# Decode attention on one core: scores by VectorE word transposes of K, a ring for all large loads, q computed first, output rows in PSUM

## The chip, the cores and the metric

The kernel runs on one core of a Trainium2 chip. The metric is the device time of one execution in microseconds (us), the median of several. The profile is one execution; its span runs from the first to the last instruction and is about 2 us shorter than the device time. A program on one core has no second die to compare with, so states were judged against the fastest run of the same kernel.

Engines are PE (matrix multiply; PEld is its weight load), DVE (VectorE), ACT (ScalarE), POOL (GpSimd) and SP, which issues nearly all loads. All loads share 16 DMA engines.

## The reference

Two branches work on `x` of shape 2 x 1 x 1024, and a gate mixes them. Nearly all bytes are in the K and V caches: 2 batches x 32 heads x 16384 keys x 128 numbers in bf16. That is 64 (batch, head) pairs, each with 4 MB of K and 4 MB of V.

```python
q = (x @ wq).reshape(B, 1, 32, 128).transpose(0, 2, 1, 3)
scores = einsum("bhqd,bhkd->bhqk", q, k_cache) * 128 ** -0.5
o = einsum("bhqk,bhkd->bhqd", softmax(scores), v_cache)
a = o.transpose(0, 2, 1, 3).reshape(B, 1, 4096) @ wo
# second branch b: layernorm, w1, gelu, token shift, w2, residual, layernorm, w3, gelu, w4, residual
g = sigmoid((x * gate_w).sum(-1, keepdims=True))
return g * a + (1 - g) * b
```

With one query per pair every byte is used once, so the time cannot fall below that of the loads.

## The kernel before

K, V and weight chunks have a pool each, K and V with two buffers. A pair's 128 score columns are split: 80 by multiplying K with a broadcast q on GpSimd (eight chunks of ten) or VectorE and reducing on VectorE, 48 by fp32 transposes on PE, copies on ACT and matmuls.

```python
kpool = ctx.enter_context(tc.tile_pool(name="kpool", bufs=2))
vpool = ctx.enter_context(tc.tile_pool(name="vpool", bufs=2))
# ... cut ...
def vec_qk_stage(i, c0, c1):
    for c in range(c0, c1):                       # CH = 8 columns a chunk; set-up cut
        if c % 4 == 3:
            nc.vector.tensor_tensor(out=prod[:], in0=Kn[:, j0 : j0 + CH, :], in1=in1, op=ALU.mult)
        else:
            nc.gpsimd.tensor_tensor(out=prod[:], in0=Kn[:, j0 : j0 + CH, :], in1=in1, op=ALU.mult)
        nc.vector.tensor_reduce(out=Ssb[:, j0 : j0 + CH], in_=prod[:], axis=AX.X, op=ALU.add)
# ... cut ...
# PV: 4 probability columns are the stationary operand, 512 columns of V move through
for g in range(NGV):                              # 32 times
    nc.tensor.matmul(o4[:], lhsT=Pt[:, 4 * g : 4 * g + 4],
                     rhs=Vf[:, 4 * g * Dh : (4 * g + 4) * Dh], start=(g == 0), stop=(g == NGV - 1))
```

The last three pairs use another PV: 128 matmuls, each with 128 x 128 of V as weights and one probability column. q is computed four heads at a time: every 8 pairs a chunk of `wq` is loaded and `compute_q_chunk` runs inside the pair loop. Of its matmuls, 16 have 512 columns; they make q broadcast over all partitions.

## Time and profile before

| | before |
|---|---|
| time, median | 1436.12 us (3 runs, 1434.21 to 1436.15) |
| span | 1434.6 us |
| bytes by the load queue | 572.55 MB |
| mean DMA rate over the span | 400 GB/s |
| busy: PE, VectorE, GpSimd | 72%, 78%, 81% |

The page of the kernel before: busy time (share of the span), the DMA rate in 40 equal slices, the load queue, and the chain of work that ended last.

```profile
span 1434.6 us, 21356 instructions
PE 1036.9 (72%) x8898; PEld 621.9 (43%) x8898; DVE 1124.5 (78%) x1357; ACT 289.9 (20%) x596; POOL 1167.5 (81%) x516
GB/s 380 305 430 421 416 272 436 430 427 423 421 423 422 429 418 411 377 417 428 422 345 424 423 417 423 349 412 423 432 410 359 421 422 417 414 362 418 423 429 169
q1 hardware_dynamic: 38376, 572.55, 95.0%
DVE 34%; POOL 34%; PE 18%; DMA 8%; issue 4%; ACT 2%; SPq 0%; ACTq 0%; DVEq 0%; POOLq 0%
```

Most slices stand at 410 to 436 GB/s, and from slice 17 on every fourth or fifth falls to 345 to 377. The chain is two thirds GpSimd and VectorE, and 8% DMA: compute is what loads wait for. One such dip in stretches of 5 us (start and end, length; busy us and number of instructions of PE, PEld, VectorE, ScalarE, GpSimd; granted clock, DMA share, GB/s):

```profile
185.00:190.00 5.00, 0.42 (x10) 0.38 (x10) 4.54 (x2) 0.00 (x0) 3.98 (x2) 0.50 0.99 426
190.00:195.00 5.00, 2.97 (x12) 1.47 (x11) 3.04 (x8) 0.49 (x2) 0.00 (x0) 0.50 0.28 115
195.00:200.00 5.00, 5.00 (x17) 1.66 (x16) 5.00 (x4) 0.00 (x0) 4.14 (x2) 0.66 0.00 0
200.00:205.00 5.00, 4.92 (x42) 2.81 (x41) 4.27 (x5) 1.09 (x3) 5.00 (x3) 1.00 0.38 105
```

For some 10 us nearly nothing is loaded, because no buffer is free. The queue's waits name whom SP waited for before it could issue (us in total, times, longest):

```profile
SPq L142 <- DVE prod L429: 664.4, 52, 29.7
SPq L142 <- POOL prod L431: 99.3, 56, 3.1
```

L142 is the K load. It waits for the last reader of the K buffer. A wait of SP costs nothing while earlier loads still fill the DMA engines; the dips show where it did cost. The groups that the costing uses (busy us, mean ns of one):

```profile
L431 POOL TENSOR_TENSOR prod<-Kn,qbc 128x1024 f32<-128x1024 bf16 x501 | 1163.0, 2356 | 216.9 <-DVE Ssb L432 155.9
L432 DVE TENSOR_REDUCE Ssb<-prod 128x8 f32<-128x1024 f32 x625 | 728.8, 1208 | 84.8 <-POOL prod L431 72.0
L429 DVE TENSOR_TENSOR prod<-Kn,qbc 128x1024 f32<-128x1024 bf16 x124 | 262.6, 2118 | 0.0
```

One PV in the old form (ns of one matmul: least, median, greatest; start of the first and the last), and a one-column PV of the last pairs (start, us, engine):

```profile
L504 PE MATMUL o_475<-Vn,Pt x32: 379/379/634, 39.8 to 49.0; 128*4 128x512 bf16 x32
1425.61 3.56 PE L535 MATMUL ocol_tail<-Pt,Vn 128*128 128x1 bf16 x128 [0.31 <-DVE OT L542]
```

### The profile page before, as it was taken

How to read it: one execution, taken by the hardware profiler on the slowest of the kernel's cores; microseconds unless marked ns; L12 is line 12 of the kernel's file. 1: busy time of each engine (PE TensorE's matmuls, PEld its weight loads, DVE VectorE, ACT ScalarE, POOL GpSimd, SP SyncE). 2: the span in 40 equal slices, each digit the busy share in tenths (PEclk: the TensorE clock that was granted, in tenths of full speed). 3: DMA queues.
4: the chain of work that ended last, by engine and by line, in shares of the span. 5: the costliest groups of instructions: out<-in, count | busy, mean ns of one | idle time of the engine just before them, and what ended most of it. 6: DMA issues, size and time to landing. Idle time of an engine off the chain costs nothing.

```text
span 1434.6 us, 21356 instructions
## 1 busy us (share of the span) xinstructions
PE 1036.9 (72%) x8898; PEld 621.9 (43%) x8898; DVE 1124.5 (78%) x1357; ACT 289.9 (20%) x596; POOL 1167.5 (81%) x516
## 2 busy tenths in 40 slices
PE   3547758867687677777588775886757867677777
PEld 2333434434343443444435443553534544354456
DVE  5688689778787875888859887788959888688863
ACT  1211212122121211211212221221212222121221
POOL 6798678888688785999959998699968999599960
PEclk7767767778777788888787887878878788777887
DMA  9799969999999999899989999899998999989994
GB/s 380 305 430 421 416 272 436 430 427 423 421 423 422 429 418 411 377 417 428 422 345 424 423 417 423 349 412 423 432 410 359 421 422 417 414 362 418 423 429 169
DMA packets 38473, 573.91 MB, mean 400 GB/s; under 512 B 3044, under 2 KB 11236, under 8 KB 21992
## 3 DMA queue, kind: packets, MB, share of 16 engines
q1 hardware_dynamic: 38376, 572.55, 95.0%
q8 instruction: 69, 1.13, 0.3%
q14 instruction: 28, 0.23, 0.0%
HBM read 572.53 MB, written 0.00 MB: 399 GB/s over the span
## 4 chain that ended last, share of the span: by engine, by line
DVE 34%; POOL 34%; PE 18%; DMA 8%; issue 4%; ACT 2%; SPq 0%; ACTq 0%; DVEq 0%; POOLq 0%
POOL prod L431 34%; DVE Ssb L432 21%; DMA Kn<-in_A_k_cache_dram 8%; DVE prod L429 7%; PE T L447 3%; DVE o4s L516 2%; PE misc L195 2%; PE misc L479 2%; PE misc L521 2%; ACT Pt L487 2%; DVE junk L482 1%; PE S L459 1%; DVE m L475 1%; PE ocol_tail L535 1%; PE o_475 L504 1%
## 5 line engine op out<-in xcount | busy, mean ns | idle before, releaser
L431 POOL TENSOR_TENSOR prod<-Kn,qbc 128x1024 f32<-128x1024 bf16 x501 | 1163.0, 2356 | 216.9 <-DVE Ssb L432 155.9
L432 DVE TENSOR_REDUCE Ssb<-prod 128x8 f32<-128x1024 f32 x625 | 728.8, 1208 | 84.8 <-POOL prod L431 72.0
L504 PEld LDWEIGHTS <-Pt 128*4 128x4 bf16 x1952 | 173.5, 91 | 321.9 <-issue 93.2
L447 PE MATMUL T<-ident_f,Kn 128*128 128x128 f32 x1596 | 311.9, 338 | 1.4 <-ACT KT L452 0.7
L452 ACT COPY KT<-T 128x512 f32<-128x512 f32 x384 | 221.9, 587 | 386.1 <-PE T L447 377.9
L429 DVE TENSOR_TENSOR prod<-Kn,qbc 128x1024 f32<-128x1024 bf16 x124 | 262.6, 2118 | 0.0
L447 PEld LDWEIGHTS T<-ident_f,Kn 128*128 128x128 f32 x1596 | 221.8, 173 | 14.8 <-issue 10.5
L459 PE MATMUL S<-qsel_122,KT 128*128 128x2 bf16 x3192 | 142.8, 166 | 48.1 <-ACT KT L452 40.1
L459 PEld LDWEIGHTS <-KT 128*128 128x128 bf16 x3192 | 130.1, 102 | 90.9 <-ACT KT L452 75.5
L477 ACT ACTIVATE Dm<-ident_f,m 128x128 f32<-128x128 f32 x64 | 25.7, 401 | 533.9 <-DVE m L475 533.9
L521 PE MATMUL misc<-ident_f,o4s 4*128 4x4 f32 x244 | 30.3, 226 | 142.7 <-DVE o4s L516 142.7
L521 PEld LDWEIGHTS misc<-ident_f,o4s 4*128 4x128 f32 x244 | 25.6, 177 | 160.8 <-DVE o4s L516 116.9
L514 DVE RECIPROCAL rinv<-misc 4x1 f32<-4x1 f32 x61 | 9.4, 154 | 86.9 <-PE misc L512 86.9
L479 PE MATMUL misc<-Dm,ones_f 128*128 128x128 f32 x128 | 42.7, 430 | 27.1 <-ACT Dm L477 27.1
L487 ACT ACTIVATE Pt<-Ssb,nb 128x128 bf16<-128x128 f32 x64 | 25.7, 401 | 154.4 <-DVE junk L482 154.4
L195 PE MATMUL misc<-wqc,x_rep 128*128 128x512 bf16 x128 | 44.1, 522 | 0.0
L179 PE MATMUL misc<-qT,sel 128*128 128x8 bf16 x16 | 1.6, 168 | 52.5 <-DVE qT L176 52.5
L479 PEld LDWEIGHTS misc<-Dm,ones_f 128*128 128x128 f32 x128 | 27.0, 262 | 28.1 <-ACT Dm L477 27.6
L482 DVE TENSOR_SCALAR_CACHE_REDUCE junk<-misc 128x128 f32<-128x128 f32 x64 | 18.6, 290 | 25.2 <-PE misc L479 25.2
L524 DVE TENSOR_REDUCE OT<-misc 128x1 bf16<-128x4 f32 x61 | 10.0, 164 | 36.0 <-PE misc L521 36.0
L512 PE MATMUL misc<-rs,ones_f 128*4 128x1 f32 x122 | 11.7, 165 | 33.2 <-ACT Pt L487 33.2
L316 PEld LDWEIGHTS <-wc 128*128 128x128 bf16 x576 | 17.8, 98 | 36.1 <-issue 35.5
(212 smaller groups left out, 771.2 us busy)
## 6 DMA issues: line engine op xcount, KB each, us to landing
Kn<-in_A_k_cache_dram SPq DMA_DIRECT2D x64, 4096.0 KB, 15.3
Vn<-in_A_v_cache_dram SPq DMA_DIRECT2D x64, 4096.0 KB, 22.5
wc<-in_B_w_dram SPq DMA_DIRECT2D x11, 1024.0 KB, 18.3
wqc<-in_A_wq_dram SPq DMA_DIRECT2D x8, 1024.0 KB, 25.9
woh<-in_A_wo_dram SPq DMA_DIRECT2D x32, 256.0 KB, 23.1
wc<-in_B_w_dram SPq DMA_DIRECT2D x8, 896.0 KB, 15.4
xr<-in_A_x_dram SPq DMA_DIRECT2D x1, 4.0 KB, 1.5
x_row<-in_A_x_dram SPq DMA_DIRECT2D x1, 4.0 KB
```

The costliest lines, as they stand in the source:

```text
L195: nc.tensor.matmul(qbps[:], lhsT=x_rep[:, b, kc, :], rhs=wqc[:, kc, :], start=(kc == 0), stop=(kc == KC - 1),)
L429: nc.vector.tensor_tensor(out=prod[:], in0=Kn[:, j0 : j0 + CH, :], in1=in1, op=ALU.mult)
L431: nc.gpsimd.tensor_tensor(out=prod[:], in0=Kn[:, j0 : j0 + CH, :], in1=in1, op=ALU.mult)
L432: nc.vector.tensor_reduce(out=Ssb[:, j0 : j0 + CH], in_=prod[:], axis=AX.X, op=ALU.add)
L447: nc.tensor.transpose(T[:, s_, :], Kn32[:, jb // 2 + s_, :], ident_f[:])
L452: nc.scalar.copy(out=KT[:], in_=T[:])
L459: nc.tensor.matmul(S[:, j0 : j0 + 2], lhsT=KTb[:, s_, :, par], rhs=qsel2[:, h, b, par, :], start=(par == 0), stop=(par == 1),)
L479: nc.tensor.matmul(R_ps[:], lhsT=ones_f[:], rhs=Dm[:], start=True, stop=True)
L482: nc.vector.tensor_scalar(out=junk[:], in0=R_ps[:], scalar1=-scale, scalar2=None, op0=ALU.mult, op1=ALU.min, accum_out=nb[:])
L487: nc.scalar.activation(out=Pt[:], in_=Ssb[:], func=ACTF.Exp, bias=nb[:], scale=scale, accum_out=rs[:])
L504: nc.tensor.matmul(o4[:], lhsT=Pt[:, 4 * g : 4 * g + 4], rhs=Vf[:, 4 * g * Dh : (4 * g + 4) * Dh], start=(g == 0), stop=(g == NGV - 1),)
L521: nc.tensor.transpose(X_ps[:, m_, :], o4s[:, m_ * Dh : (m_ + 1) * Dh], ident_f[0:4, 0:4])
```

## The change

The intent is to take GpSimd and the broadcast q out of the scores. VectorE transposes K in 32 x 32 blocks of 32-bit words (two bf16 numbers each), and PE multiplies the blocks with a q that is masked so that each of 8 chunks lands in its own rows of one PSUM tile. All q is computed before the loop, all large loads go through one ring of 5 slots, PV is the one-column form everywhere, and the output projection and the second branch are accumulated as rows in PSUM. Bytes from memory stay the same.

```diff
-    kpool = ctx.enter_context(tc.tile_pool(name="kpool", bufs=2))
-    vpool = ctx.enter_context(tc.tile_pool(name="vpool", bufs=2))
+    big = ctx.enter_context(tc.tile_pool(name="big", bufs=5))
 ... (cut: weight loads, constants, all q before the loop, masks)
+        for m in range(NM):                        # 8 chunks
+            T = tpool.tile([P, 2, CJ, 32], FP32, name="T")
+            nc.vector.transpose(
+                out=T[:].rearrange("p w j s -> p j w s"),
+                in_=Kw[:, m * CW : (m + 1) * CW].rearrange("p (j w e) -> p j w e", w=2, e=32),
+            )
+            for v in range(4):
+                nc.tensor.matmul(
+                    S[:],                          # 128 x 512, accumulated over m and v
+                    lhsT=z[:, v, 7 - m : 7 - m + P],
+                    rhs=Tb[:, v // 2, :, v % 2],
+                    start=(m == 0 and v == 0),
+                    stop=(m == NM - 1 and v == 3),
+                )
 ... (cut: softmax with a second VectorE transpose, of P)
+        for j in range(NJ):                        # 128
+            nc.tensor.matmul(
+                oc[:],
+                lhsT=V[:, j, :],
+                rhs=PT[:, j % CJ, j // CJ : j // CJ + 1],
+                start=(j == 0),
+                stop=(j == NJ - 1),
+            )
 ... (cut: rows in PSUM, second branch)
     for i in range(NPAIR):
+        build_z(i + 2)
+        qk_stage(i)
+        softmax_stage(i)
+        pv_stage(i)
 ... (cut)
+        issue_v(i + 2)
+        issue_k(i + 3)
```

## The prediction

> **What bounds it now.** Page, part 3: 572.5 MB through one queue in 1434.6 us, 399 GB/s on average. Cutting the span into 5 us windows, the 135 windows whose DMA share is 1.0 or more move a mean 434.7 GB/s; at that rate the bytes take 1317 us. So loads could hide everything, but the queue starves: the queue's waits show K loads held 664 us (52 times) by VectorE's multiply, and windows near 60, 195, 575, 745, 915, 1085 and 1255 us fall to 0-160 GB/s. Those dips recur every 8 pairs, where a wq chunk comes and its q work sits in the chain. The chain of waits is POOL 34%, DVE 34%: the K*q multiply (2.36 us on GpSimd, 2.12 us on VectorE, both per 1024 elements) and the reduce (1.21 us) make the pair's pace about 21 us, against 19.3 us for its 8.39 MB at 434.7 GB/s.
>
> **What the change does per pair.** Removed: about 8 GpSimd multiplies, 2 VectorE multiplies, 10 reduces, fp32 PE transposes and their ACT copies, and PV with 32 matmuls of 512 columns (8.2-9.5 us). Bytes do not change.
> Added, estimates from the trace:
> - 8 VectorE 32x32 transposes of 128x1024 f32. The Trainium skill ("Vector Engine (DVE) Microarchitecture Reference", 3.8) says transposes sustain one element per cycle per lane, so I take the pace of the 1024-element reduces back to back: 1.15 us, together 9.3 us. No transpose runs before, so the trace does not test this.
> - 32 matmuls of 512 columns: 216 ns warm, 427 ns cold. The skill ("TensorE: Matmul & The Clock Gate", Part 1) has the clock rise only after a busy window of about 3.4 us; the trace agrees roughly: PV starting at 39.8 us sees clock 0.50 until about 44.9, then 1.00. They follow the transposes, cost about 1.1 us after the last, plus about 0.4 us of stall while cold (three T buffers).
> - Softmax: max of 512 from PSUM 0.7, PE transpose 0.4, small max 0.3, matmul 0.6, copy 0.2, exp 0.7, 32x32 transpose of P 0.7: about 3.8 us with handoffs.
> - PV as 128 one-column matmuls: the old tail's three ran 128 in 3.4-3.6 us, warm or cold.
> - Scaling 0.25 us.
>
> VectorE waits for PV before the next pair's transposes, so the pair is one serial loop: 9.3+1.5+3.8+3.7+0.3 = about 18.7 us, just below DMA (19.6 us with wo). The ring lets loads run up to three tiles ahead.
>
> **Sum.** First load about 2 us, 1317 us of loads, then the last pair after its loads and output (old end, from last scaling, 5.4 us): about 15 us. That is 1334 if loads never starve. The second branch adds perhaps 55-80 us of in-line PE/DVE work against 43 us of its loads, in pairs 6-34; the ring should absorb most, I add 12 us. Predicted 1346 us, range 1322 to 1400. Faster by over 2% 0.86, within 2% 0.07, slower 0.07.
>
> **What would show each step.** DMA rate about 430 GB/s in nearly every slice, no periodic dips; POOL nearly idle; VectorE about 60-65% busy; VectorE transpose mean 1.15-1.25 us; PV about 3.5 us per pair; K loads' waits short; the chain ending through DMA or the VectorE loop; PE clock alternating 0.5 and 1.0.
>
> **What would make it wrong.** A 4-byte transpose at half rate (2.2 us) makes the loop 27 us: about 1750 us. PE cold throughout makes QK 13.7 us: about 1500. Strided weight loads in the second branch slow enough to drain the ring: +20 to 60 us. A loop of 20.5 us instead of 18.7: about 1400, compute-bound.

## The result and the profile after

| | before | after |
|---|---|---|
| time, median | 1436.13 us (4 runs, 1434.2 to 1441.4) | 1362.33 us (4 runs, 1362.0 to 1362.8) |
| span | 1434.6 us | 1360.1 us |
| mean DMA rate | 400 GB/s | 422 GB/s |
| VectorE, GpSimd busy | 78%, 81% | 55%, 2% |
| mean granted PE clock | 0.793 | 0.745 |

The ratio is 0.9475 (95% interval 0.9454 to 0.9496). The lines of the page that answer to those above, and the small queue q8 that fetches instructions (packets, MB, share of 16 engines' span):

```profile
span 1360.1 us, 24487 instructions
PE 968.4 (71%) x11196; PEld 527.5 (39%) x11260; DVE 748.2 (55%) x948; ACT 51.7 (4%) x132; POOL 33.8 (2%) x79
GB/s 401 437 422 433 431 428 432 426 430 429 430 427 432 429 428 430 431 427 428 432 432 425 429 431 430 426 432 427 432 428 431 428 429 431 427 428 432 427 426 170
q1 hardware_dynamic: 24628, 572.54, 98.3%
q8 instruction: 88, 1.44, 0.4%
DMA 68%; PE 19%; DVE 9%; issue 3%; ACT 1%; DVEq 0%; POOL 0%; ACTq 0%
```

The dips are gone: 38 of 40 slices stand at 422 to 437 GB/s. The chain is now 68% DMA. Two stretches at the former dip:

```profile
190.00:195.00 5.00, 2.93 (x69) 2.60 (x70) 1.62 (x5) 0.78 (x2) 0.26 (x1) 0.72 0.99 421
195.00:200.00 5.00, 3.23 (x73) 2.06 (x71) 1.88 (x3) 0.00 (x0) 0.00 (x0) 0.50 0.99 423
```

VectorE's own waits show which way the wait now runs, and the lines after them are the new transpose (512 of them), one whole pair without its wait for K, from its first transpose to the scaling of its output, and the PV of the pair before it:

```profile
DVE OT L316 <- PE oc L309: 226.1, 64, 3.6
DVE T L260 <- DMA Kn<-in_A_k_cache_dram: 110.6, 59, 9.8
```

```profile
L260 DVE STREAM_TRANSPOSE T<-Kn 128x1024 f32<-128x1024 f32 x512 | 595.9, 1216 | 135.4 <-DMA Kn<-in_A_k_cache_dram 110.6
```

```profile
53.25:71.49 18.24, 13.88 (x164) 7.53 (x164) 11.48 (x14) 0.78 (x2) 0.48 (x1) 0.78 1.00 428
48.18 3.51 PE L309 MATMUL oc<-PT,Vn 128*128 128x1 bf16 x128 [0.36 <-DVE rinv L306]
```

In 59 pairs VectorE waits for K, 1.9 us each on average (110.6 / 59). This pair's loop takes 18.24 us (all 64: 17.7 to 18.9 us, median 18.1), shorter than the time of its loads (8.39 MB at the 431 GB/s of e1 below: 19.5 us), so compute waits. The first of the two waits shows the serial nature of the loop: VectorE stands still for 3.5 us (226.1 / 64) in every pair while PV runs.

The end of the run is the part that was not foreseen:

```profile
1320.00:1330.00 10.00, 9.54 (x31) 3.52 (x30) 8.02 (x8) 0.00 (x0) 0.00 (x0) 0.73 1.02 432
1330.00:1335.00 5.00, 2.80 (x64) 2.47 (x65) 1.75 (x5) 0.78 (x2) 0.00 (x0) 0.72 0.68 288
1335.00:1340.00 5.00, 2.60 (x77) 2.20 (x76) 2.35 (x3) 0.00 (x0) 0.00 (x0) 0.50 0.51 213
1340.00:1345.00 5.00, 5.00 (x18) 1.91 (x18) 4.79 (x6) 0.00 (x0) 0.00 (x0) 0.75 0.49 200
```

From 1335 us the loads run at half rate, DMA share 0.5, although all of them had been issued by 1311 us. Seven of the 16 DMA engines had finished by 1332.5 us. The trace also holds the times at which each load's semaphore was raised: once by each of the 16 engines, when its part has landed. For single tiles of the kernel after (us):

```
                 first    8th      9th      last     first to last
wq, first half   12.53    12.71    12.75    13.20     0.67
a K tile        174.95   176.06   176.48   178.23     3.27
a K tile        552.72   556.62   558.80   560.52     7.80
a V tile        935.08   941.99   945.93   947.64    12.56
last V piece   1330.49  1340.23  1345.98  1348.25    17.75
```

The engines drift apart through the whole run: the queue never runs dry, so nothing makes the fast ones wait for the slow ones. In the kernel before, the spread stayed below 5 us in all 188 loads whose 16 completions stand clear of others: each dip lets all engines finish. It is not that the kernel before fetched fewer instruction pages: e5 below, which keeps its dips, fetched 113 against 88 here, and its spread was at most 6.4 us. A tile is used when its last part has landed: that of the last K landed at 1337.84 us, and its first transpose began at 1337.87.

### The profile page after: what moved, and what is told of

It is laid out like the page before. It is cut to its first block, busy times and chain, and to the rows that moved or that the text cites. A ratio compares the mean times of both kernels' runs of the same rounds, so it can differ in the third digit from the quotient of the medians.

```text
span 1360.1 us, 24487 instructions
## 1 busy us (share of the span) xinstructions
PE 968.4 (71%) x11196; PEld 527.5 (39%) x11260; DVE 748.2 (55%) x948; ACT 51.7 (4%) x132; POOL 33.8 (2%) x79
## 3 DMA queue, kind: packets, MB, share of 16 engines
q1 hardware_dynamic: 24628, 572.54, 98.3%
## 4 chain that ended last, share of the span: by engine, by line
DMA 68%; PE 19%; DVE 9%; issue 3%; ACT 1%; DVEq 0%; POOL 0%; ACTq 0%
DMA Kn<-in_A_k_cache_dram 66%; PE S L268 12%; DVE T L260 6%; PE oc L309 5%; DMA x_pm<-in_A_x_dram 2%; ACT Pr L290 1%; DVE PT L294 1%; DVE m L279 1%; PE misc L285 1%; PE misc L212 1%; DVE mx L283 0%; PE misc L281 0%; PE misc L412 0%; DVE nb L287 0%; DVE x_row L437 0%
## 5 line engine op out<-in xcount | busy, mean ns | idle before, releaser
L260 DVE STREAM_TRANSPOSE T<-Kn 128x1024 f32<-128x1024 f32 x512 | 595.9, 1216 | 135.4 <-DMA Kn<-in_A_k_cache_dram 110.6
L268 PE MATMUL S<-T,z_141 128*128 128x512 bf16 x682 | 203.8, 453 | 61.1 <-DVE T L260 55.4
L309 PEld LDWEIGHTS <-Vn 128*128 128x128 bf16 x8192 | 231.7, 103 | 24.6 <-issue 24.6
L309 PE MATMUL oc<-PT,Vn 128*128 128x1 bf16 x8192 | 224.2, 165 | 20.3 <-DVE rinv L306 18.1
L268 PE MATMUL S<-T,z_143 128*128 128x512 bf16 x651 | 196.4, 457 | 58.7 <-DVE T L260 53.4
L268 PE MATMUL S<-T,z_145 128*128 128x512 bf16 x651 | 193.7, 452 | 60.6 <-DVE T L260 55.3
L268 PEld LDWEIGHTS <-z_141 128*128 128x128 bf16 x704 | 78.1, 111 | 186.6 <-issue 132.3
L268 PEld LDWEIGHTS <-z_143 128*128 128x128 bf16 x672 | 75.2, 112 | 180.5 <-issue 130.8
L268 PEld LDWEIGHTS <-z_145 128*128 128x128 bf16 x672 | 74.4, 111 | 181.3 <-issue 129.5
L316 DVE TENSOR_SCALAR OT<-oc,rinv 128x1 bf16<-128x1 f32 x64 | 14.1, 221 | 226.1 <-PE oc L309 226.1
L290 ACT ACTIVATE Pr<-S,nb 128x512 bf16<-128x512 f32 x64 | 44.0, 687 | 1246.7 <-DVE nb L287 1246.7
L279 DVE TENSOR_REDUCE m<-S 128x1 f32<-128x512 f32 x64 | 44.2, 691 | 74.6 <-PE S L268 74.6
L304 PE MATMUL misc<-rs,quarter_f 128*128 128x1 f32 x128 | 27.3, 283 | 71.6 <-ACT Pr L290 71.6
L294 DVE STREAM_TRANSPOSE PT<-Pr 128x512 bf16<-128x512 bf16 x64 | 45.5, 711 | 57.8 <-ACT Pr L290 57.8
L285 PE MATMUL misc<-mx,nscale_f 1*128 1x1 f32 x128 | 24.2, 256 | 23.8 <-DVE mx L283 23.8
L285 PEld LDWEIGHTS misc<-mx,nscale_f 1*128 1x128 f32 x128 | 18.7, 183 | 36.0 <-DVE mx L283 36.0
L283 DVE TENSOR_REDUCE mx<-misc 1x1 f32<-1x128 f32 x64 | 17.8, 278 | 23.2 <-PE misc L281 23.2
```

What stands on the lines that cost most here:

```text
L260: nc.vector.transpose(out=T[:].rearrange("p w j s -> p j w s"), in_=Kw[:, m * CW : (m + 1) * CW].rearrange("p (j w e) -> p j w e", w=2, e=32),
L268: nc.tensor.matmul(S[:], lhsT=z[:, v, 7 - m : 7 - m + P], rhs=Tb[:, v // 2, :, v % 2], start=(m == 0 and v == 0), stop=(m == NM - 1 and v ...
L279: nc.vector.reduce_max(out=m[:], in_=S[:], axis=AX.X)
L283: nc.vector.reduce_max(out=mx[:], in_=mT[:], axis=AX.X)
L285: nc.tensor.matmul(nb_ps[:], lhsT=nscale_f[:], rhs=mx[:], start=True, stop=True)
L290: nc.scalar.activation(out=Pr[:], in_=S[:], func=ACTF.Exp, bias=nb[:], scale=scale, accum_out=rs[:])
```

## The experiments

Twelve more kernels ran. The comparison with the reference passed in all of them, also where the arithmetic was wrong (e2 uses one K tile for all pairs): the scores hardly show in the output at this tolerance, so a pass is no proof of them. Theory A: the load stream bounds the kernel after, and most of the gain came from the dips of before. Rival B: the compute loop still starves the ring.

### e1: loads only

```diff
-        for m in range(NM):
+        for m in range(1):
-        for j in range(NJ):        # PV
+        for j in range(4):
 ... (cut: the stop flags that go with them)
```

> The kernel after with an eighth of the K transposes and score matmuls and 4 of 128 PV matmuls per pair; every load as before (wrong result on purpose). Theory A: the time after is that of the load stream, and what the ring costs is little: 1335 to 1352 us, and the spread between the first and the last of the 16 completions of the last tile is again above 12 us (after: 17.8 us), so the drift belongs to the DMA engines. Rival B: the compute loop (18.3 us a pair plus the second branch) starves the ring now and then and costs the difference between 428 and 435 GB/s: then this kernel takes 1325 us or less.

Measured: 1341.29 us. Its rate between 5 and 1330 us and its instruction pages:

```profile
5.00:1330.00 1325.00, 311.08 (x1506) 148.23 (x1524) 230.62 (x483) 49.72 (x129) 32.30 (x70) 0.60 1.00 431
q8 instruction: 12, 0.20, 0.1%
```

With compute nearly gone the stream runs at 431 GB/s, not 435, and the time is only 21 us below the kernel after: B falls. But the spread of the last tile was 4.2 us, not above 12. The part of theory A that gave the drift to the DMA engines alone fell too; compute has a hand in it.

### e2: compute only

One K and one V tile were loaded and used by all pairs.

```diff
     def issue_k(i):
+        if i >= 1:
+            kn_tiles[i] = kn_tiles[0]
+            return
 ... (cut: the same for V, and pools for the two tiles)
```

> One K tile and one V tile are loaded and used by all 64 pairs; weights are loaded as before, the arithmetic is that of the kernel after (wrong result on purpose). Theory A (loads bound the kernel after): the serial loop is about 18.4 us a pair: 34 + 64 x 18.4 + about 50 for the second branch = 1262, so 1240 to 1290 us. Rival B (compute binds): 1340 us or more.

Measured: 942.16 us, far below both numbers. The order of the instructions shows why this run is no measure of the loop of after: here the next pair's transposes of K (L267) run between the softmax steps of this one (L301) and during its PV, which in the kernel after they never do.

```profile
500.66 1.21 DVE L267 STREAM_TRANSPOSE T<-Kn 128x1024 f32<-128x1024 f32 x1
501.81 0.66 DVE L301 STREAM_TRANSPOSE PT<-Pr 128x512 bf16<-128x512 bf16 x1
503.02 2.35 DVE L267 STREAM_TRANSPOSE T<-Kn 128x1024 f32<-128x1024 f32 x2
503.83 3.34 PE L316 MATMUL oc<-PT,Vn 128*128 128x1 bf16 x128
```

About 14.2 us a pair ((942 - 34) / 64, the second branch included) is what that order needs. It says that compute in another order would be far under the loads. The loop of the kernel after is better read from its own trace, 18.24 us.

### e3: PV in the old form

```diff
-        for j in range(NJ):
-            nc.tensor.matmul(oc[:], lhsT=V[:, j, :], rhs=PT[:, j % CJ, j // CJ : j // CJ + 1], ...)
+        for j in range(0, NJ, 4):
+            nc.tensor.matmul(o4[:], lhsT=PT[:, j % CJ : j % CJ + 4, j // CJ], rhs=V[:, j : j + 4, :], ...)
+        # then scale, four 4 x 128 transposes and the sum of the diagonal, as in the kernel before
```

> The kernel after with PV undone: 32 matmuls of 4 columns by 512 and the collection of the diagonal, as before. If the pair is one serial loop on VectorE, the loop grows from 18.3 by about 9 - 3.5 + 1.5 to 25 us, beyond the 19.6 us of the loads: about 34 + 64 x 25 + 50 = 1690 us (1560 to 1720), slower than the kernel before. Rival: PV hides behind the loads, and the time stays under 1400 us.

Measured: 1620.78 us, 13% slower than the kernel before, and inside the range. PE's mean granted clock was higher (0.908), so this is not a clock effect. It shows in this kernel that PV's length lies on the path: the serial loop stays under the loads only with the short form.

### e4: the kernel before without the q work in the loop

```diff
     def compute_q_chunk(c, wqc):
+        if c > 0:
+            return
-        qbc = qbc_tiles[h // HG]
+        qbc = qbc_tiles[0]
```

> The kernel before with all wq chunks loaded but only the first computed; all heads use the first chunk's broadcast q (wrong result on purpose). If the periodic dips of the DMA rate come from the q work in the chain, seven of about 7 us are gone: about 1385 us (1370 to 1400). Rival: the pace of the GpSimd and VectorE scores binds by itself and the dips only show it: 1420 us or more.

Measured: 1389.63 us, 46 us less than before, as theory A had it. Its slices in the page:

```profile
GB/s 392 297 422 424 420 348 437 425 427 421 432 420 426 424 427 413 420 418 431 413 428 429 430 431 423 429 431 428 430 424 429 429 429 414 436 428 430 429 429 170
```

The dips from slice 17 on are gone. Two stay, so they were not q work alone. In slice 6, near 190 us, the layernorm of the second branch stands in the chain (6.75 us on VectorE). In slice 2, near 60 us, it is the first pair's own PV (9.4 us) and GpSimd's multiplies; with the short PV of e5 this slice rises from 305 to 369 GB/s.

### e5: the kernel before with one-column PV in all pairs

```diff
-        if is_tail(i):
-            return pv_stage_tail(i)
+        return pv_stage_tail(i)
```

> The kernel before with PV as 128 one-column matmuls for all pairs: one part of the change alone. [...] a PV of 3.5 instead of 8 to 9.5 us lets the score transposes and the q work start sooner; but GpSimd and VectorE set the pace of a pair (34% each of the chain), so the gain is small: 1405 to 1432 us. If PE's waits were the main loss, it would come near 1380.

Measured: 1403.14 us, 33 us less than before and slightly better than the expected range. PE's granted clock fell from 0.793 to 0.591, and the kernel was still faster.

### e12: both edits of e4 and e5

> The kernel before with both edits of e4 (q work of chunks 1 to 7 left out, -46 us) and e5 (one-column PV, -33 us); wrong result on purpose. If the two add up, it comes to 1357 to 1364 us, the time of the kernel after, and the old scores on GpSimd, VectorE and PE were fast enough for the load stream by themselves. If GpSimd and VectorE's pace (about 21 us a pair) bound it, 1375 us or more.

Measured: 1378.04 us: 57.5 us gained, where the sum is 79. The chain by engine, and GpSimd's group:

```profile
POOL 41%; DMA 35%; DVE 14%; PE 6%; issue 2%; ACT 1%; SPq 0%; POOLq 0%; DVEq 0%; ACTq 0%
L433 POOL TENSOR_TENSOR prod<-Kn,qbc 128x1024 f32<-128x1024 bf16 x501 | 1167.9, 2365 | 169.1 <-DMA Kn<-in_A_k_cache_dram 114.4
```

GpSimd's multiply still leads the chain, but it waits 114 us for K: both limits are close. The new scores, with all else in the change, are worth the rest against this version, 15.7 us (1378.04 - 1362.33). Taken last, as here, they are the largest part of the diff and the smallest part of the gain; no run puts them into the kernel before by themselves.

### e9 and e10: who makes the DMA engines drift

The kernel after has 88 instruction pages of 16 KB, 1.07 us each in the median. Their durations in order of time repeat with period 8 (autocorrelation 0.89 at a lag of 8, and at most 0.34 at smaller lags), so I read them as going round 8 of the 16 engines. Theory C: those 8 engines fall behind by these pages. Rival D: engines fall behind because compute reads SBUF. e9 is e1 with the whole PV put back, many instructions and little PE time. e10 is e1 with the scores put back, few instructions and much PE and VectorE time.

```diff
# e9, against the kernel after
-        for m in range(NM):
+        for m in range(1):
 ... (cut: the stop flag)
# e10, against the kernel after
-        for j in range(NJ):        # PV
+        for j in range(4):
 ... (cut: the stop flag)
```

> e1 with the whole PV put back (128 one-column matmuls a pair, about 16,000 more PE instructions; 3.5 us of PE work a pair). Theory C: the drift of the 16 DMA engines comes from instruction fetch: pages of 16 KB of 1.07 us each, which go round 8 of the 16 engines. About 72 pages instead of 12 make 9 a fetching engine: the spread of the last tile's completions is 11 to 15 us (e1: 4.2) and the last load lands 7 to 9 us later than in e1 (1335.5), near 1343. Rival D: the drift comes from compute reading SBUF while loads are written: PV is short, and the spread stays below 8 us.

> e1 with all eight transposes and 32 score matmuls put back, PV at 4 of 128 (wrong result on purpose). PE and VectorE read SBUF for some 10 us a pair, three times as long as PV in e9, but PE has only 6,202 instructions, about 24 pages or 3 a fetching engine. Theory C: spread of the last tile 5 to 7 us, last load near 1337. Rival D (SBUF reads): spread above 12 us, more than in e9.

Measured: e9 1353.22 us, e10 1351.84 us. The completions of the last V piece (us):

```
         pages   first    7th      8th      9th      15th     last
e1        12   1330.63  1332.11  1332.36  1332.37  1333.98  1334.84
e10       26   1330.53  1332.16  1335.13  1335.27  1336.91  1340.40
e9        74   1330.40  1332.07  1334.54  1344.28  1344.75  1346.10
after     88   1330.49  1331.84  1340.23  1345.98  1347.74  1348.25
```

The first seven engines finish between 1330.4 and 1332.2 us in all four: nothing in compute slows them. Eight others fall behind together: the 9th to 16th in e9 and the kernel after, the 8th to 15th in e10. Their mean lies 4.2 us (e10), 13.6 (e9) and 16.4 (after) behind that of the first seven. For the pages fetched by then, 25, 72 and 85, shared by 8 engines, that is 1.3 to 1.5 us a page. So the delay grows with the pages, as theory C has it, and a page costs its engine somewhat more than the 1.07 us of its own record. That is why C's sizes were short in e9: a spread of 11 to 15 us was expected and 15.7 measured, and a landing 7 to 9 us later than in e1 and 11.3 measured.

In e10 the spread of 9.9 us is above C's 5 to 7 and below D's 12, so both miss. The excess is a single engine, 3.5 us behind the next. The kernel after has one too: the 8th, at 1340.23 us, as late as the last in e10; in e9 the 8th comes at 1334.54. So the score work delays one engine by some 6 us more (my reading, since the records do not name engines) and not all of them, which speaks against SBUF reads in general. Both runs with the full score work also have six more small instruction blocks of 8 KB on another queue (15 against 9), but at 0.3 us each these are too short by themselves. What delays this engine stays open.

### e8: moving bytes from one half of the DMA engines to the other

```diff
+        if i in (16, 32, 48):
+            for p0, pn in [(0, 96)] + [(96 + 8 * a, 8) for a in range(4)]:
+                nc.sync.dma_start(out=tv[p0 : p0 + pn], in_=src[p0 : p0 + pn])
```

> The kernel after; three of the 64 V loads are cut into a transfer of 96 partitions, which takes 16 engines, and four of 8 partitions, which the Trainium skill says take the lowest-numbered 8 engines: 6 rows of 32 KB (1.21 us each) more for each of those and 6 fewer for the other 8. If the pages are fetched by the other 8, the spread of the last tile falls from 17.8 us to 3 to 8 us, the last load lands near 1342 instead of 1348, and the time is 1354 to 1358 us (after: 1362.3). If the low 8 fetch them, the spread grows to about 30 us and the time to 1368 to 1372. If drift has nothing to do with halves, nothing moves.

(The passage meant is in "DMA: Bandwidth & Descriptors", section "Why a DMA increments its semaphore by 16 and not by 1".)

Measured: 1467.16 us, slower than the kernel before. None of the three outcomes came. The page's rate shows a hole at each of the three tiles, and SP's waits show loads held by the landing of earlier loads:

```profile
GB/s 404 431 434 424 431 431 427 429 429 381 204 431 427 430 429 428 432 429 429 367 167 367 431 428 430 430 427 430 431 312 185 376 430 430 427 430 428 429 413 39
SPq L129 <- DMA Kn<-in_A_k_cache_dram: 48.0, 2, 26.6
SPq L99 <- DMA Vn<-in_A_v_cache_dram: 74.5, 9, 19.9
```

At the end 13 of the 16 completions of a last load lay within 8 us, and the last three came 11.7, 19.5 and 28.0 us after the first. Each small transfer did use 8 engines (the load queue has 96 packets more than in the kernel after for 12 of them, 24724 against 24628), but the delay is not spread evenly over 8. Which engines fetch instructions stays open.

### e6: four ring slots

```diff
-    big = ctx.enter_context(tc.tile_pool(name="big", bufs=5))
+    big = ctx.enter_context(tc.tile_pool(name="big", bufs=4))
```

> The kernel after with 4 ring slots instead of 5. One slot less takes about 10 us off how far loads run ahead. If the fifth slot only covers the pairs that carry second-branch work (6 to 34), the rest of the run is unchanged and the time is 1364 to 1385 us; if the stream needs it in every pair (SP waits for a slot before each load), each pair loses some us: over 1420 us. With fewer loads queued the DMA engines can drift less: spread of the last tile below 12 us (after: 17.8).

Measured: 1362.27 us, the same as with five (1362.33), and the spread of the last tile was again 17.1 us. Both parts of the expectation missed: the time was to be 1364 us or more and the spread below 12. The fifth slot buys nothing, and one slot fewer does not hold the engines together.

### e7 and e11: shortening the end

e7 cuts the last K load into four pieces. e11, shown here, also halves the K loads of pairs 48 to 62.

```diff
+        step = NJ // 4 if i == NPAIR - 1 else NJ // 2 if i >= 48 else NJ
+        for j0 in range(0, NJ, step):
+            nc.sync.dma_start(out=tk[:, j0 : j0 + step, :], in_=ks[:, j0 : j0 + step, :])
```

> The kernel after with the last K load cut into 4 pieces. Its transposes could start at the first piece, but pair 62 holds VectorE until 1337.0 us, less than 1 us before that K has landed whole (1337.8): gain under 2 us, 1360 to 1363 us. If the landing of the last K alone sets the tail, 1354 to 1357.

> The kernel after with K loads of pairs 48 to 62 in two halves and the last in four pieces. VectorE idles 1.3 to 2 us a pair for K; halves let each pair start up to 4.9 us earlier, so over these pairs the loop catches up by up to 4.9 us and pair 63 is ready for PV when the last V piece lands (1348.3): 1353 to 1358 us, faster than the kernel after (1362.3). If more DMAs on 8 semaphores hold SP back, 1362 us or more.

Measured: e7 1360.80 us, e11 1357.39 us; both as expected. e11 is the fastest version with its arithmetic left whole: 0.9442 of before, 5 us less than the kernel after. Its last pair begins here, against 1337.87 us in the kernel after (start, us):

```profile
1332.95 4.61 DVE L261 STREAM_TRANSPOSE T<-Kn 128x1024 f32<-128x1024 f32 x4
```

## Why the prediction held, and where its terms were off

The predicted 1346 us stood against 1362.33 us measured, inside the range.

1. **What bound the kernel before** was right. e4 shows the q work in the chain at 46 us. The prediction took every dip for q work, and two were more than that: the one near 195 us belongs to the second branch at least in part, the one near 60 us to the first pairs' PV and multiplies. That PV's length cost the kernel before 33 us (e5) was not in the prediction.
2. **The pair's loop** was right: 18.7 us predicted, 18.24 in the trace; transposes 1.216 us each in the mean (1.15 to 1.25 predicted), PV about 3.5 us. VectorE was busy 55% of the span, a little under the 60 to 65% predicted. A transpose of 4-byte words ran at the pace of a reduce of as many elements, as the prediction took from the Trainium skill, "Vector Engine (DVE) Microarchitecture Reference", section 3.8; this trace agrees in so far as the two take the same time (1216 and 1208 ns for 1024 elements a partition); it does not count cycles.
3. **The load term was mis-sized.** "That is 1334 if loads never starve" took 434.7 GB/s from the 5 us windows with DMA share at or above 1.0. Choosing windows by a noisy share picks the high ones: in e1, whose stream never starves and runs at 431 GB/s from 5 to 1330 us, the 5 us windows with a share at or above 1.0 give a mean of 439. In e1 the last V piece landed at 1334.8 us, against 1319 (2 + 1317) predicted: +15.8 us, of which the rate is 11 (572.5 MB at 431 GB/s take 1328 us) and the rest the slow first microseconds and e1's own spread of 4.2 us.
4. **The further drift was missing.** It delays the last V piece from 1334.8 (e1) to 1348.3 us: +13.4 us. The profile of the kernel before hardly shows it, because its dips undo the drift (spread below 5 us).
5. **The second branch was over-sized.** "I add 12 us" was not paid: the rate from 5 to 1330 us is 429 GB/s against 431 in e1, no slice dips, and the fastest DMA engine finishes at 1330.5 us as it does there: -12 us.
6. **The end** was 11.8 us after the last V piece (1360.1 - 1348.3), 15 predicted: -3.2 us.

The sum 1346 + 15.8 + 13.4 - 12 - 3.2 gives 1360.0, the span measured (it must, as each term is taken from the measured times; the device time is 2.2 us longer, for which the prediction had no term). The terms in points 3 and 5 nearly cancel, so the closeness of the total owes something to chance; that loads would bound the kernel, and by about what margin, does not.

Of 73.8 us gained, the kernel before could have had 57.5 (e12) by taking the q work out of the loop and using one-column PV. That part is an upper mark, since e4 and e12 leave the q work out instead of moving it. VectorE's transposes, with everything else, account for the remaining 15.7 us (the two don't add to 73.8 exactly: in e12's rounds the kernel before took 1435.55 us). The drift takes back 13.4 us of what the steady loads could have given.

## What to carry to other kernels

Where loads should bound a kernel, look first for work that enters the loop only now and then: a periodic dip in the DMA rate points at it, and one run without that work prices it. Measure the load floor with a run that keeps every load and almost no compute, not by picking the best windows of a trace. When a queue never runs dry, compare the first and the last of a load's completions near the end of the run: engines that drift apart cost time that a mean busy share hides.

## What the Trainium skill lacked or had wrong

- "DMA: Bandwidth & Descriptors", section "Where 436 GB/s comes from", says that the HBM side (about 358 GB/s per core) binds HBM to SBUF transfers, though it also calls a measured 425 GB/s near the fabric's rate. e1 sustained 431 GB/s for 1325 us on one core. "HBM Reference", section "Specifications (TRN2)", which expects about 425 GB/s for a core that streams alone, is close to it.
- "Runtime: NRT & Kernel Launch", section "Terms", says that instruction memory is refilled in 16 KiB blocks; this trace agrees (88 packets of 16 KB). "DMA: Bandwidth & Descriptors", section "Queues, rings and completion order", names refill among the queue rows that share the 16 engines (row 14; the large blocks stand under queue 8 here), but neither page gives the time of a block (1.07 us) or says that under a full queue the engines drift apart (17.8 us within 1350 us). Section "Instruction fetch mechanics" of the Runtime page calls the cost of a block "mostly hidden"; in e9, with 62 blocks more than in e1, the last V piece landed 11.3 us later.
- "TensorE: Matmul & The Clock Gate", Part 1, ties the clock to PE activity. It does not say that dense one-column matmuls do not raise it: two PVs of this form in a row, 1421.8 to 1429.2 us in the kernel before, ran at clock 0.5 throughout, where the wide PV begun at 39.8 us came to 1.0 at about 44.9. With them in all pairs (e5) the mean granted clock fell from 0.793 to 0.591. It hardly matters to them: in e5 the 128 matmuls of a PV took 3.4 us in the mean at clock 1.0 and 3.6 at 0.5.
- "DMA: Bandwidth & Descriptors", section "Why a DMA increments its semaphore by 16 and not by 1", says that an HWDGE transfer over k engines takes the lowest-numbered k. In e8, transfers of 8 partitions left three engines 11.7 to 28.0 us behind the first instead of splitting two halves. Records do not name engines, so this is unresolved rather than refuted.
